# A two-stage block with linear attention and a gated layer: mask, zero products, shifts, numerators and the written-out order changed together

## The chip, the cores and the metric

One Trainium2 chip, one of its cores. The metric is the device time of one execution in microseconds (us), the median of several runs. The core has five engines that run their own instruction queues: TensorE (PE), VectorE (DVE), ScalarE (ACT), GpSimd (POOL) and SyncE (SP), which here issues nearly all DMAs. Matmul results go to PSUM, eight banks of 512 fp32 columns; everything else lives in SBUF.

## The reference

Input `x` is 2048 rows of 640 (bf16). First linear attention with 32 heads of 20 columns, then a bilinear gated layer, each behind a LayerNorm without weights and with a residual. Cut to what matters:

```python
def _A_ref(x, wqkv, w_phi, wo):
    qkv = (x @ wqkv).reshape(B, S, 3, H, Dh).transpose(2, 0, 3, 1, 4)
    q, k, v = qkv[0], qkv[1], qkv[2]
    pq = einsum("bhsd,hdf->bhsf", q, w_phi)
    pk = einsum("bhsd,hdf->bhsf", k, w_phi)
    phi_q = concatenate([softmax(pq), softmax(-pq)], -1)
    phi_k = concatenate([softmax(pk), softmax(-pk)], -1)
    kv = einsum("bhsf,bhsd->bhfd", phi_k, v)
    z = einsum("bhsf->bhf", phi_k)
    num = einsum("bhqf,bhfd->bhqd", phi_q, kv)
    den = einsum("bhqf,bhf->bhq", phi_q, z)[..., None] + 1e-6
    return (num / den).transpose(0, 2, 1, 3).reshape(B, S, D) @ wo
h = x + _A_ref(layernorm(x), A_wqkv, A_w_phi, A_wo)
n = layernorm(h)
out = h + ((n @ B_w_gate) * (n @ B_w_up)) @ B_w_down
```

## The kernel before, in words

**Tiles.** The 2048 rows are 16 tiles of 128. Names of operations carry the tile: `K7` is the key projection of tile 7.

**How the order is set.** `build_graph` makes some thousand operations, each with its engine, reads and writes. Nothing is scheduled at run time: the table `PLAN` gives each operation a due time, which sorts its engine's queue, an optional choice of engine (`:1` or `:2`, an index into the alternatives named at the operation), and the slot that it takes in a pool of buffers (PSUM banks for matmuls). The entry `xn3:12.223:1:2` means: tile 3's normalised rows, twelfth microsecond, second choice of engine, slot 2. `emit` sets the semaphore waits that the order and the reuse of slots ask for. An instruction that waits holds up all behind it on its engine.

**Opening.** PE first runs ten products of zeros, 512 columns each (L365), of which eight touch one PSUM bank each. Meanwhile SP loads `x1`, `x0` and the five row blocks `wk0` to `wk4` of the key weight. GpSimd builds the identity (`id0`, `id1`, L324 and L327) and the block mask `GL`, which tells for each of 128 rows of a weight chunk which head it belongs to: a memset (L325) and two selections for each of the five chunks (`gla`, `glb`, L333 and L336), ten in all. `Ph0` to `Ph2` (L374) multiply the small matrix `w_phi` with that mask into the block matrix Phi. PE transposes the key weight (`WT0` to `WT4`, L386), multiplies it with Phi (`F1_0` to `F1_4`, the folds, L405), and the folded weight then makes features straight from rows. Evacuations from PSUM are `WTe`, `Fe`, `xte`, `Ve` (L245), on ScalarE or VectorE.

**Rows.** Per tile: statistics (`L1s`, `L1a`, VectorE), one over the deviation by logarithm and exponential (`L1l`, `L1e`, ScalarE, for groups of 1, 1, 2, 4, 4 and 4 tiles), the shift -mean times that (`L1n`, L437, one instruction per tile, on GpSimd or VectorE, from tile 2 on), the normalised rows (`xn`, L445 on ScalarE or L447 on VectorE), and their transposition (`xt`: tiles 0 to 3 on PE, L456, the others by a transposing DMA on SP, L465). Tiles 0 and 1 have their projections cut into five pieces by weight block (`V0_0` to `V0_4`).

**Keys and values.** `V` and `K` (L476), two exponentials of plus and minus the product (`Kx`, L488), sums (`Ks`), reciprocals by `Kr` and `Ke`, the product that normalises (`Kn`, GpSimd, L512, 1280 columns), and `KV` (L520), eleven matmuls per tile that gather over all tiles in two PSUM banks. `KVe` masks them into `KVm`.

**Queries.** `wqt` transposes the query weight from memory by DMA, `F0` folds it, and `Q` makes the products; `Qx` the exponentials (L545 and L547) into one of six slots of `ph`; `Qs`, `Qr`, `Qb`, `Qe` the sums and their ratio; `Qn` (GpSimd, L564, 660 columns); `qT` (SP, L569) transposes `ph` and frees its slot when it has landed.

**Numerators.** `N` (L582): eleven matmuls per tile, three heads each, 63 columns (the last 42): 20 numerators and the denominator per head. Groups 0 to 5 lie in one bank, 6 to 10 in another. `dd` and `rd` (L593, L596) make the reciprocal denominators, `o` (L599) the quotients, both as two halves of 18 heads, which is 36 or 720 columns. `oT` transposes by DMA, `O` (L609) multiplies with the output weight, `h` (L615) adds the residual, `hc` centres it, `hT` transposes it.

**Gated layer.** Blocks of 256, 512, 512, 512 and 256 rows: `U` (L652) twice per 128 columns of the inner width, `g` and `u` (L657, L660), `D` (L671), `y` (L683) and the write `w` (L685). The last tile, 15, has its `D` and `y` cut by columns at 320 and 512 (`LASTCUT`).

```python
G.op("pe", "N%d" % t, nf, mm_c(*[21 * n for n in BH]), LT, [phT] + kvm_b, [b], kk)
...
G.op("sp", "qT%d" % t, lambda e, ph=ph, phT=phT: e.dma_start_transpose(
    out=T["phT"][:, phT.slots[0], :, :], in_=T["ph"][:, ph.slots[0], :]), 1.5, 0.0, [ph], [phT], kk, dma=-2.3)
```

Of the kernel before, what the change touches and what calls it, by code (L numbers as in the profile page):

```python
# [32 lines left out]

NB = 11
# [8 lines left out]
NWARM = 10  # L43
LASTCUT = [(0, 320), (320, 512), (512, 640)]
# [4 lines left out]
gl0:0.78 gla2:0.942 phz:1.084 eps:1.8 gla3:1.83 glb3:2.059 zero:0.91 w5:0.78 gla1:2.198 warm0:1.239 x1:0.78 id0:2.34 gla0:2.484 glb2:2.626 gla4:2.765 L1s1:3.188  # L49
L1a1:4.098 L1l1:4.331 x0:1.26 L1s0:4.207 L1a0:5.117 L1e1:4.657 glb4:2.994 xn1:5.226::0 Ph2:3.223 glb0:3.817 glb1:3.955 Ph0:4.184 wk2:1.74:1 L1l0:5.35 L1e0:5.676  # L50
xn0:5.914::1 warm1:1.665 warm2:2.091 warm3:2.517 Ph1:4.778 warm4:2.943 warm5:3.369 warm6:3.795 wk0:2.22:1 x2:2.7 warm7:4.221 warm8:4.647::0 wk1:3.18 warm9:5.077
id1:5.17 WT2:5.52::0 WTe2:6.139 WT0:5.958::1 WTe0:6.724 xt1:6.375::2 xt0:6.654::3 xte0:7.309 F1_2:6.933::4 WT1:7.252::6 WTe1:7.894:1 wk3:3.66 WT3:7.669::7
L1s2:6.426 Fe1_2:7.45 WTe3:8.289 xte1:8.697:1 F1_0:8.086::0 Fe1_0:8.603:1 wk4:4.14:1 WT4:8.405::3 WTe4:9.104:1 F1_1:8.822::4 Fe1_1:9.339 x3:4.62:1 x6:5.1
L1s3:9.512 L1a2:10.3 F1_3:9.141::6 Fe1_3:9.923 va1:5.414 L1a3:10.422 K0_0:9.46::0 L1s6:10.531 F1_4:9.731::2 Fe1_4:10.507:1 L1s7:11.319 wv0:5.58:1 V0_0:10.1::4
wv1:6.06 L1l2:11.091 x4:6.54 K0_1:10.371 K0_2:10.642 L1e2:11.417 L1s5:12.105 ekz:6.244 L1n2:11.697 V1_0:10.913::6 V1_1:11.184 L1n3:11.921 xn3:12.223:1:2
L1s4:12.893 L1a4:13.803 L1a7:13.912 K1_0:11.455::2 x12:7.02 wv2:7.5:1 K1_1:11.726 K0_3:11.997 wv4:7.98:1 L1a5:14.021 xn2:14.13::3 K1_2:12.268 K1_3:12.539
K1_4:12.81 V0_1:13.081 Kx1_0:13.28::0 Kx1_1:13.864 V1_2:13.352 wv3:8.46 wu1:8.94 L1a6:14.642 wg4:9.42 V0_2:13.623 V0_3:13.894 V0_4:14.165 wqt4:9.9 Ve0:14.635::0
V1_3:14.436 xt3:14.707::2 xte3:15.184:1 L1l4:15.219 L1e4:15.545 L1n5:15.825 K0_4:14.986 x8:11.21 Kx0_0:15.638::1 Kx0_1:16.222 Ks1:15.592::0 L1n4:16.049
V1_4:15.257 xt2:15.528::3 K3:15.807::4 Ve1:16.806::1 L1n7:16.985:1 L1n6:16.273 xn6:17.39:1:0 Kr1:18.195 V3:17.163::0 Ke1:18.486 Kn1:18.82 xn4:18.632:1:1
xn7:19.437:1:2 x10:11.69 wqt0:12.17 Ve3:20.242::2 xn5:17.16::3 xt5:17.785 rqz:21.133 xte2:17.672:1 L1s9:18.081 L1s11:18.867 Kx3_0:20.826::2 Kx3_1:21.41  # L60
# [24 lines left out]
V15:71.666::2 Ve15:73.222::5 KV12:73.022 KV13:73.355 KV14:73.688 KV15:74.021 KVe1:74.555 Qb5:73.403 Qe5:73.806 Qr13:73.925::2 Qn5:74.113 Q7:74.354::0
KVe0:74.805 N1:75.721::6 qT5:76.245::0 dd1:76.252::0 rd1:76.467 N0:76.054::2 o1:76.881::0 Q14:76.387::4 Qb13:75.378 Qe13:75.653 Qx7_0:75.919::0 Qx7_1:76.529
dd0:77.692::0 rd0:77.907 Qn13:75.96 oT1:77.808::0 qT13:79.118::1 N3:77.754::0 dd3:78.285::1 rd3:78.5 o0:78.79::1 o3:79.601::2 oT0:80.608::1 oT3:81.918::2
Q11:78.087::6 Qx11_0:79.652::5 Q8:79.746::2 Qx11_1:80.262 Qs7:80.412 N2:81.113::0 dd2:81.847::0 rd2:82.062 Qx14_0:80.872::1 Qx14_1:81.482 O1:81.446::6
o2:82.476::0 oT2:83.403::3 h1:83.287 Qr7:82.092::0 Qb7:82.436 N9:82.804::4 dd9:84.107::0 rd9:84.322 o9:84.736::1 Q12:83.432::0 Qe7:82.711 Qx8_0:83.328::2
N5:84.799::6 dd5:85.547::0 rd5:85.762 o5:86.176::2 Qx8_1:83.938 hc1:84.548::3 O0:85.132::2 h0:86.987 hc0:87.932::2 O3:86.49::4 h3:88.047 N4:87.848::6  # L90
dd4:88.867::0 L2q1:88.65 rd4:89.082 o4:89.496::0 Qn7:83.018 qT7:84.713::4 Qx12_0:89.49::0 Qr6:90.1::1 L2v1:90.307:1 oT9:86.203::0 L2q0:90.246 O2:88.181::2
hT1:87.513 Qb6:90.444 Qe6:91.086 Q15:89.539::4 O9:90.906::6 Qx12_1:91.205 N7:92.264::0 h2:90.392 Qs8:91.212 Qn6:91.393 h9:92.647 dd7:93.467::0 rd7:93.682
# [139 lines left out]
def build_graph():  # L232
# [341 lines left out]
    for t in range(NT):  # L574
# [13 lines left out]
        def nv(b, lo, hi):  # L588
            return pp(b, 0, 378).rearrange("p b (h e) -> p b h e", e=21)[:, :, :, lo:hi]
# [323 lines left out]
```

## Time and profile before

| | us |
|---|---|
| median of three runs (272.31 to 272.6) | 272.32 |
| the profiled execution | 272.55 |
| its span, first to last instruction | 270.8 |
| first product of zeros starts | 1.25 |
| first transposition of a weight starts | 6.03 |
| last matmul ends | 268.28 |

The granted TensorE clock is 1.00 in the whole span. All times below that are given as points are us from the start of the span of the profiled execution. A row of the page or of a stage shows the busy time of each engine and the number of its instructions; a row of a group shows busy time, the mean duration of one instruction in ns, and then the idle time of its engine just ahead of it with what ended that. PE's matmuls overlap: a matmul of 320 columns lasts about 0.30 us in the records, but the next starts 0.136 us after it.

### The profile page before, as it was taken

How to read it: one execution, taken by the hardware profiler on the slowest of the kernel's cores; microseconds unless marked ns; L12 is line 12 of the kernel's file. 1: busy time of each engine (PE TensorE's matmuls, PEld its weight loads, DVE VectorE, ACT ScalarE, POOL GpSimd, SP SyncE). 2: the span in 40 equal slices, each digit the busy share in tenths (PEclk: the TensorE clock that was granted, in tenths of full speed). 3: DMA queues.
4: the chain of work that ended last, by engine and by line, in shares of the span. 5: the costliest groups of instructions: out<-in, count | busy, mean ns of one | idle time of the engine just before them, and what ended most of it. 6: DMA issues, size and time to landing. Idle time of an engine off the chain costs nothing.

```text
span 270.8 us, 5184 instructions
## 1 busy us (share of the span) xinstructions
PE 266.0 (98%) x2103; PEld 177.1 (65%) x2103; DVE 161.6 (60%) x295; ACT 123.8 (46%) x304; POOL 72.8 (27%) x98
## 2 busy tenths in 40 slices
PE   7999999999999999999999999999999999999996
PEld 3877787777777689865656747775445457544774
DVE  4989999989689978887754434223123312424224
ACT  3999999788846667232254443003213510032000
POOL 8124989999942222331000000000000000000000
DMA  6997899967947989589347032041000000100003
GB/s 185 323 249 159 128 299 329 146 140 134 196 91 149 131 180 157 62 167 120 59 91 105 0 73 51 0 69 30 29 0 15 0 0 27 69 5 1 2 24 104
DMA packets 66600, 27.76 MB, mean 103 GB/s; under 512 B 57744, under 2 KB 65296, under 8 KB 66576
## 3 DMA queue, kind: packets, MB, share of 16 engines
q1 hardware_dynamic: 65120, 26.42, 47.3%
q10 hardware_dynamic: 1456, 1.01, 1.6%
q8 instruction: 16, 0.26, 0.4%
q14 instruction: 8, 0.07, 0.1%
HBM read 11.00 MB, written 2.62 MB: 50 GB/s over the span
## 4 chain that ended last, share of the span: by engine, by line
PE 90%; DVE 3%; DMA 3%; ACT 2%; POOL 1%; issue 0%; SPq 0%; DVEq 0%; POOLq 0%
PE ps L652 38%; PE ps L476 22%; PE ps L671 19%; PE ps L609 6%; PE ps L520 2%; DMA scratch<-ph 2%; PE ps L582 1%; DVE o L599 1%; PE ps L405 1%; DMA w<-in_A_w_phi_dram 1%; DVE sm L596 1%; ACT scratch L245 1%; POOL Phi L374 1%; DVE S L550 1%; ACT ph L545 0%; ACT ek L626 0%
## 5 line engine op out<-in xcount | busy, mean ns | idle before, releaser
L652 PE MATMUL ps<-xnT,Wgu 128*128 128x512 bf16 (+1 forms) x600 | 107.0, 336 | 0.0
L652 PEld LDWEIGHTS ps<-xnT,Wgu 128*128 128x128 bf16 x600 | 58.1, 98 | 43.4 <-DVE ev L660 0.4
L657 ACT ACTIVATE gt<-ps 128x512 bf16<-128x512 f32 (+1 forms) x60 | 29.0, 510 | 94.2 <-PE ps L652 90.4
L476 PE MATMUL ps<-Wp,xnT 128*128 128x320 bf16 (+1 forms) x480 | 68.8, 299 | 0.3 <-DVE o L599 0.2
L660 DVE TENSOR_TENSOR ev<-ps,gt 128x512 bf16<-128x512 f32 (+1 forms) x60 | 33.3, 580 | 41.7 <-PE ps L652 28.8
L476 PEld LDWEIGHTS ps<-Wp,xnT 128*128 128x128 bf16 x480 | 45.5, 97 | 18.3 <-DVE o L599 0.7
L671 PE MATMUL ps<-Wd,ev 128*128 128x320 bf16 (+2 forms) x396 | 53.3, 295 | 0.0
L671 PEld LDWEIGHTS ps<-Wd,ev 128*128 128x128 bf16 x396 | 38.1, 98 | 14.8
L512 POOL TENSOR_TENSOR ek<-ek,SR 128x1280 bf16<-128x1280 bf16 x16 | 37.5, 2357 | 4.0 <-ACT SR L497 3.9
L683 DVE SCALAR_TENSOR_TENSOR Wp<-ps,rs,x_all 128x640 bf16<-128x640 f32 (+3 forms) x18 | 14.4, 807 | 38.2 <-PE ps L671 38.1
L550 DVE TENSOR_REDUCE S<-ph 128x66 f32<-128x1320 bf16 x16 | 24.0, 1521 | 3.5 <-ACT ph L547 3.4
L630 POOL TENSOR_SCALAR ln<-mv 128x1 f32<-128x1 f32 x8 | 1.5, 190 | 89.3 <-ACT ek L626 88.9
L492 DVE TENSOR_REDUCE SR<-ek 128x64 f32<-128x1280 bf16 x16 | 23.3, 1478 | 1.2 <-ACT ek L488 1.0
L609 PE MATMUL ps<-Wo,Wp 128*128 128x320 bf16 x160 | 24.0, 299 | 0.0
L564 POOL TENSOR_TENSOR ph<-ph,RQ 128x660 bf16<-128x660 bf16 x16 | 20.8, 1306 | 10.2 <-ACT RQ L560 10.0
L545 ACT ACTIVATE ph<-ps 128x600 bf16<-128x600 f32 x32 | 21.2, 679 | 4.3 <-PE ps L476 3.6
L488 ACT ACTIVATE ek<-ps 128x640 bf16<-128x640 f32 x32 | 21.1, 701 | 0.5 <-PE ps L476 0.5
L609 PEld LDWEIGHTS ps<-Wo,Wp 128*128 128x128 bf16 x160 | 15.4, 98 | 6.7
L615 DVE SCALAR_TENSOR_TENSOR x_all<-ps,x_all 128x640 bf16<-128x640 f32 x16 | 13.1, 820 | 9.3 <-PE ps L609 9.2
L599 DVE TENSOR_TENSOR o<-ps,sm 128x720 bf16<-128x720 f32 x16 | 14.4, 903 | 1.3 <-DVE sm L596 0.5
L626 ACT ACTIVATE ek<-x_all,mv 128x640 bf16<-128x640 bf16 x16 | 13.1, 821 | 2.8 <-DVE x_all L615 2.8
L624 ACT ACTIVATE xn<-x_all,mv 128x640 bf16<-128x640 bf16 x10 | 8.2, 825 | 9.5 <-DVE x_all L615 9.5
(64 smaller groups left out, 166.3 us busy)
## 6 DMA issues: line engine op xcount, KB each, us to landing
out_dram<-Wp SPq DMA_DIRECT2D x15, 160.0 KB, 1.9
x_all<-in_A_x_dram SPq DMA_DIRECT2D x6, 320.0 KB, 6.1
Wgu<-in_B_w_up_dram SPq DMA_DIRECT2D x5, 384.0 KB, 6.4
Wgu<-in_B_w_gate_dram SPq DMA_DIRECT2D x5, 384.0 KB, 4.1
Wd<-in_B_w_down_dram SPq DMA_DIRECT2D x2, 480.0 KB, 6.8
Wd<-in_B_w_down_dram ACTq DMA_DIRECT2D x2, 480.0 KB, 4.5
ev<-in_A_wqkv_dram SPq DMA_DIRECT2D x5, 160.0 KB, 3.8
Wp<-in_A_wqkv_dram SPq DMA_DIRECT2D x5, 160.0 KB, 5.9
```

The costliest lines, as they stand in the source:

```text
L476: ins = e.matmul(pb(b, hb)[:, 0:n1 - n0], lhsT=T["xnT"][:, NC - 1 - c, P * t:P * (t + 1)], rhs=T["Wp"][:, POS[kind], c, n0:n1], start=(c = ...
L488: G.op("act", "%sx%d_%d" % (nm, t, s), lambda e, s=s, b=b, ek=ek: e.activation(out=T["ek"][:, ek.slots[0], 0:2 * D].rearrange("p (b h s f) ...
L492: G.op("dve", "%ss%d" % (nm, t), lambda e, ek=ek, sr=sr: e.tensor_reduce(out=T["SR"][:, sr.slots[0], 0, :], in_=T["ek"][:, ek.slots[0], 0: ...
L512: G.op("pool", "Kn%d" % t, lambda e, eng, ek=ek, sr=sr: e.tensor_tensor(out=T["ek"][:, ek.slots[0], 0:2 * D].rearrange("p (h f) -> p h f", ...
L545: e.activation(out=v[:, 0:10].rearrange("p (b g) j f -> p b g j f", b=2), in_=pp(b, 0, 300).rearrange("p b (g j f) -> p b g j f", j=3, f=D ...
L550: G.op("dve", "Qs%d" % t, lambda e, t=t, ph=ph: e.tensor_reduce(out=T["S"][:, t, 0:66].rearrange("p (g k) -> p g k", k=6), in_=pv(ph).rear ...
L564: return e.tensor_tensor(out=v, in0=v, in1=T["RQ"][:, rq.slots[0], 1, 0:33].rearrange("p (g j) -> p g j", j=3).unsqueeze(3).to_broadcast([ ...
L609: ins = e.matmul(pb(b, hb)[:, 0:320], lhsT=T["oT"][:, oT.slots[0], c, :], rhs=T["Wo"][:, c, 320 * hb:320 * (hb + 1)], start=(c == 0), stop ...
L652: ins = e.matmul(pb(b)[:, 0:n], lhsT=T["Wgu"][:, gu, c, P * ft:P * (ft + 1)], rhs=T["xnT"][:, NC - 1 - c, o0:o0 + n], start=(c == 0), stop ...
L657: G.op("act", "g%d_%d" % (bi, ft), lambda e, pg=pg, gt=gt, n=n: e.activation(out=T["gt"][:, gt.slots[0], 0:n], in_=pb(pg)[:, 0:n], func=AF ...
L660: o_ = G.op("dve", "u%d_%d" % (bi, ft), lambda e, pu=pu, gt=gt, hh=hh, ft=ft, n=n: e.tensor_tensor(out=T["hh"][:, hh.slots[0], ft, 0:n], i ...
L671: ins = e.matmul(pb(b, hb)[:, 0:w], lhsT=T["hh"][:, hh.slots[0], ft, P * tt:P * (tt + 1)], rhs=T["Wd"][:, ft, c0 + w * hb:c0 + w * (hb + 1 ...
```

## The change

Seven things change together.

1. The mask gets one layout for all chunks, nine columns per chunk (`GW`), and is made by a memset and two selections over all 45 columns; the products that make Phi read the columns that they need from it.
2. The zero products are 256 columns wide instead of 512: eight that touch the banks and fourteen more (`NFILL`), the last two of them among the first transpositions. The memset that they read is half as large.
3. The shift `L1n` is one VectorE instruction per group of tiles instead of one instruction per tile on GpSimd or VectorE.
4. The numerators of group g start at column 64 g of two neighbouring banks (eight groups in the first, three in the second), and `dd`, `rd` and `o` run over 11 groups of three heads: 33 instead of 36, and 660 instead of 720 columns.
5. `xn` may run on GpSimd; `PLAN` puts tiles 2, 3, 4, 7, 9, 11 and 13 there. Before, 3, 4 and 7 were on ScalarE and the others on VectorE.
6. The last tile is cut at 320 and 576 instead of 320 and 512; its middle part, now 256 columns, is still the last matmul group of all.
7. `PLAN` is new from end to end: due times, slots and some choices of engine for evacuations, loads and the second LayerNorm.

The diff, cut; of `PLAN` the lines of the opening and those around tile 7's transposition:

```diff
+GW = 9
...
-NWARM = 10
-LASTCUT = [(0, 320), (320, 512), (512, 640)]
+NFILL = 14
+LASTCUT = [(0, 320), (320, 576), (576, 640)]
...
-dd4:88.867::0 L2q1:88.65 rd4:89.082 o4:89.496::0 Qn7:83.018 qT7:84.713::4 Qx12_0:89.49::0 Qr6:90.1::1 L2v1:90.307:1 oT9:86.203::0 L2q0:90.246 O2:88.181::2
-hT1:87.513 Qb6:90.444 Qe6:91.086 Q15:89.539::4 O9:90.906::6 Qx12_1:91.205 N7:92.264::0 h2:90.392 Qs8:91.212 Qn6:91.393 h9:92.647 dd7:93.467::0 rd7:93.682
...
+xt1:6.093::2 xte1:6.571 xn0:6.114::1 gl0:1.526 gla:1.688 wk1:2.22 wk2:2.7:1 WT1:6.372::3 WT2:6.651::4 xt0:6.93::5 glb:1.992 Ph2:2.585 Ph0:3.179 WTe2:7.154
+WTe0:6.644:1 Ph1:3.773 F1_0:7.209::6 Fe1_0:7.739:1 WTe1:7.052 warm21:7.528 F1_1:7.637::0 Fe1_1:8.323 wk4:3.18:1 WT4:7.956::2 x3:3.66:1 wk3:4.14 WT3:8.235::3
...
+V1_0:11.639::2 K0_2:11.91 K0_3:12.181 wv1:6.54 V0_1:12.452 K0_4:12.723 V1_1:12.994 L1a6:14.56 wv2:7.02:1 V0_2:13.265 Kx0_0:13.193::1 Kx0_1:13.777 Ks0:14.669::0
+xn2:11.908:2:2 xt2:13.536::4 wv3:7.5 V0_3:13.815 x10:7.98 wv4:8.46:1 V0_4:14.086 xte2:14.361 xn3:13.008:2:3 L1l4:14.945 L1e4:15.271 L1n4:16.062 xn5:16.296::0
...
+Qe7:82.235 Qn7:82.542 Q15:84.24::4 qT7:84.321::0 oT9:85.811::0 N5:85.607::2 dd5:86.138::0 rd5:86.353 Qx14_0:84.421::1 Qx14_1:85.031 N4:85.94::6 dd4:86.643::1
+hc1:85.641::0 hT1:87.121 o5:86.767::2 Q12:86.273::0 O2:87.664::2 hc0:86.359::2 hT0:88.431 rd4:87.522 o4:87.936::0 Qx12_0:88.531::4 Qx12_1:89.141 Qs8:88.691
+Qr8:90.244::3 Qb8:90.588 Qe8:90.863 oT4:89.741::1 h2:90.126 Qn8:91.17 O3:89.022::6 hc2:91.071::1 h3:90.946 O9:90.38::0 h9:91.937 N7:91.738::2 dd7:92.757::0
...
-    for c in (0, 4, 1, 2, 3):
-        lo, n, o = CH[c][0], NH[c], OFF[c]
-        base = P * c - DH * lo
-        k = -97 if c in (0, 4) else -80
-        G.op("pool", "gla%d" % c, lambda e, n=n, o=o, base=base: e.affine_select(
-            out=T["GL"][:, o:o + n], in_=T["GL"][:, o:o + n], compare_op=ALU.is_ge, fill=0.0, base=base,
-            pattern=[[-DH, n]], channel_multiplier=1), 0.22, LP, [gl_b[c]], [gl_b[c]], k)
...
+    G.op("pool", "gla", lambda e: e.affine_select(
+        out=T["GL"][:, :, :], in_=T["GL"][:, :, :], compare_op=ALU.is_ge, fill=0.0, base=0, pattern=[[P - 6 * DH, NC], [-DH, GW]],
+        channel_multiplier=1), 0.24, LP, [gl_b], [gl_b], -97)
+    G.op("pool", "glb", lambda e: e.affine_select(
+        out=T["GL"][:, :, :], in_=T["GL"][:, :, :], compare_op=ALU.is_ge, fill=0.0, base=DH - 1,
+        pattern=[[6 * DH - P, NC], [DH, GW]], channel_multiplier=-1), 0.24, LP, [gl_b], [gl_b], -96.5)
...
+    for k in range(8):
+        G.op("pe", "warm%d" % k, lambda e, k=k: e.matmul(T["PS"][:, 512 * k:512 * k + 256], lhsT=T["zero"][:, 0:P],
+             rhs=T["zero"][:, :], start=True, stop=True), 0.11, LT, [z_b], [], -90,
+             before=[G.by["warm%d" % j] for j in range(k)])
...
-                G.op("pool", "L1n%d" % t, lambda e, eng, t=t: e.tensor_scalar(
-                    out=T["nb"][:, t:t + 1], in0=T["mv"][:, t, 0:1], scalar1=T["rs"][:, t:t + 1], scalar2=-1.0, op0=ALU.mult,
-                    op1=ALU.mult), 0.2, LP, [rs_b[t], mv_b[t]], [nb_b[t]], 10 * t - 25, alts=[("dve", 0.07, LD)])
+        if z > 2:
+            G.op("dve", "L1n%d" % a, lambda e, a=a, z=z: e.scalar_tensor_tensor(
+                out=T["nb"][:, a:z], in0=T["mv"][:, a:z, 0], scalar=-1.0, in1=T["rs"][:, a:z], op0=ALU.mult, op1=ALU.mult), 0.075, LD,
+                [rs_b[t] for t in tl] + [mv_b[t] for t in tl], [nb_b[t] for t in tl], 10 * a - 25)
...
-             alts=[] if t < 2 else [("act", act_c(640, True), LA)])
+             alts=[] if t < 2 else [("act", act_c(640, True), LA), ("pool", 1.15, LP)])
...
-                y, h0, h1 = g // 6, 3 * g, 3 * g + BH[g]
-                ins = e.matmul(pb(b, y)[:, 21 * (h0 - 18 * y):21 * (h1 - 18 * y)], lhsT=T["phT"][:, phT.slots[0], g, :],
+                y, h0, h1 = g // 8, 3 * g, 3 * g + BH[g]
+                ins = e.matmul(pb(b, y)[:, 64 * (g % 8):64 * (g % 8) + 21 * BH[g]], lhsT=T["phT"][:, phT.slots[0], g, :],
...
-            out=T["o"][:, o.slots[0], :].rearrange("p (b h d) -> p b h d", b=2, d=DH), in0=nv(b, 0, 20),
-            in1=smv(sm, 1).unsqueeze(3).to_broadcast([P, 2, 18, DH]), op=ALU.mult), dve_c(720, True), LD, [b, sm], [o], kk)
+            out=T["o"][:, o.slots[0], 0:33 * DH].rearrange("p (g j d) -> p g j d", j=3, d=DH), in0=nv(b, 0, 20),
+            in1=smv(sm, 1).unsqueeze(3).to_broadcast([P, NB, 3, DH]), op=ALU.mult), dve_c(660, True), LD, [b, sm], [o], kk)
```

In the new `PLAN`, PE's order from Q7 on is Q7, N1, N0, Q11, N3, Q8, N2, N9, Q14, O1, O0, Q15, N5, N4, Q12, O2, O3, O9, N7, U0. ScalarE's around it: Qx7 twice, Qr10, the first half of Qx11, Qr6, Qe6, the second half of Qx11. SP's: qT5, oT1, oT0, qT13, oT3, oT2, qT7, oT9, hT1, hT0. SP's loads at the start: x1, x0, wk0, wk1, wk2, wk4, x3, wk3, x2, wv0, x6, x4, wv1, wv2, wv3, x10, wv4 (x6, x4 and x10 are two tiles each); before: x1, x0, wk2, wk0, x2, wk1, wk3, wk4, x3, x6, wv0, wv1, x4, x12, wv2, wv4, wv3.

## The prediction

> **What bounds the kernel now.** First the page's busy times, then TensorE (PE) by stages, from the first transposition of a weight (6.03) to the end of the last matmul. In each row the figure after the comma is PE's busy time.
>
> ```profile
> PE 266.0 (98%) x2103; PEld 177.1 (65%) x2103; DVE 161.6 (60%) x295; ACT 123.8 (46%) x304; POOL 72.8 (27%) x98
> ...
> 6.03:16.57 10.54, 10.47 (x115) 8.32 (x116) 9.28 (x27) 8.94 (x19) 1.73 (x4) 1.00 1.15 299
> 16.57:76.89 60.32, 60.32 (x605) 45.16 (x603) 54.37 (x68) 53.26 (x141) 51.01 (x46) 1.00 0.83 188
> 76.89:94.40 17.51, 16.85 (x189) 12.22 (x186) 16.28 (x34) 10.68 (x30) 4.22 (x5) 1.00 0.87 138
> 94.40:268.29 173.89, 173.88 (x1194) 110.03 (x1194) 78.49 (x161) 48.90 (x112) 10.82 (x21) 1.00 0.30 55
> ```
>
> PE is full in the second and fourth row, and there the matmuls start at their own pace: 136 ns apart for 320 columns, 216 for 512, 31 for 63. Busy time hides waits shorter than a matmul's 0.2 to 0.6 us, so I read the start of every matmul and took the pace off. After 6.03 about 2.1 us are lost: 0.25 in WT0, 0.24 before F1_1, 0.16 before V0_0, 0.16 before V0_3, then 0.27 before Q8, 0.37 before Q12, 0.55 before N7 and 0.12 before U0; 0.2 more is spread over 2000 matmuls. Only four places can be shortened: the start, the opening, the stage around 77 to 94, and what follows the last matmul (2.5 us). The chain of waits names them:
>
> ```profile
> 5.64 0.26 POOL ident L327
> 5.90 0.14 issue
> 6.03 0.70 PE ps L386 x5
> ...
> 86.03 5.30 DMA scratch<-ph
> 91.33 0.02 issue
> 91.35 0.67 ACT ph L545
> ...
> 268.38 0.42 DVE Wp L683
> ```
>
> The start hangs on GpSimd (POOL), which makes the identity last, after ten selections and three products. Later one transposition of feature rows, qT7, takes 5.30 us; only then is its `ph` slot free for Qx12, which must empty the banks that N7 needs. The last write ends the program.
>
> **Sum against the profiled execution:** it took 272.55 us, of which 270.8 are the span; the median of the runs shown is 272.32. I work out a difference in the span and take it off the median.
>
> **The opening.** Ten selections become two (L333/L336 took 0.19 to 0.20 us for 7 or 8 columns, the mask's L353 0.31 for 33; two times 0.2 to 0.31), and id0, id1, eps and `ekz` (0.62) come ahead, `phz` (0.84) and `va1` (1.23) behind Phi. So the identity is ready near 2 instead of 5.89. Phi's three products (1.8) still wait for w5, landed at 3.47, and end near 5.3. The zero products: 22 of 256 columns instead of 10 of 512. The ten started 0.427 us apart, half the full pace, so 20 take 4.27 and end near 5.4 (they start 0.12 earlier, the memset being half as large). Then WT0 needs wk0, now third on SP's queue; the third landing was at 5.28. So dense work starts near 5.45, 0.58 earlier. The two last zero products (0.1 to 0.2 each) fall into gaps: xt1 still waits for xn1 on VectorE (DVE), which ended at 6.20.
>
> I don't book 0.58, because **what is late next** is weights. SP's order changes, but the queue delivers one 160 KB tile per 0.4 to 0.9 us: the 20th landed at 14.60 (wv3, which V0_3 waited for). In the new order the 20th is wv4, for V0_4. PE alone gets there at about 14.2: 5.45, five WT and two xt at 0.28 (2.0), xt2 (0.28), five folds at 0.32 (1.6), sixteen projection pieces at 0.272 (4.35), zero products 0.3, and about 0.25 at half pace. Waits of up to 0.4 (Fe1_1 behind four evacuations of 0.59 on ScalarE) are thus covered; beyond that they cost in full. V0_4 at 14.66, four pieces (1.09) and xt3 (0.28) give V2 at 16.03. The same work was done before at K3, 16.57: **-0.54** (0 to -0.95).
>
> **Rows on GpSimd.** Seven `xn` (2, 3, 4, 7, 9, 11, 13) go there from ScalarE (0.92 each) and DVE (0.55 to 0.60). No such row exists. From below: GpSimd's tensor-scalar of one column, 0.19. From above: its product of 1280 columns.
>
> ```profile
> L512 POOL TENSOR_TENSOR ek<-ek,SR 128x1280 bf16<-128x1280 bf16 x16 | 37.5, 2357 | 4.0 <-ACT SR L497 3.9
> L564 POOL TENSOR_TENSOR ph<-ph,RQ 128x660 bf16<-128x660 bf16 x16 | 20.8, 1306 | 10.2 <-ACT RQ L560 10.0
> ```
>
> The nearest row, 660 columns, makes 1.27 for 640; I take that. xn2 can start near 12.3, after DVE's new shift; xt2 may come at 14.1 and xt3 at 15.75 without delaying V0_4 or V2, so 1.7 each is free, behind V0 and V1 on PE. The other five queue among the Kn products. From 16.57 to 76.89 GpSimd is idle for 9.3 us, 3.9 of it early, waiting for ScalarE before a Kn; ten L1n (0.27 each) leave, so 8.0 can be used, and five rows take 6.4. Booked at nothing; if that cover goes, KV15 is late by the rest. Four shifts of about 0.2 go to DVE, which PE didn't wait for there.
>
> From 16 to 76 I book **0**: same matmuls, no PE wait before, evacuations at similar distances. The tightest spot is F0_1, which needs wqt0: SP reaches it after xt5 (near 17.5; 1.3), x14 (0.6) and five more transpositions (1.3 each), near 25.9; wqt1 took 4.1 us to land, so 30.0. Ten projections at 1.36 and two KV at 0.34 from V2's start put F0_1 at 30.3.
>
> **The stage at 77 to 94.** Numerators at a stride of 64 leave N's eleven matmuls as they are; o shrinks from 720 to 660 columns (0.903, less 60 columns at 1.25 ns: 0.83), rd and dd by three columns (0.02). Nine tiles: 0.8 of the 16.28 us that DVE is busy. Bounds: -0.8 to 0 (the pattern gains a dimension; the old one also crossed a bank); I take 0, since the SP queue, not DVE, is late here. Before, 1.31 were lost. In the new order N9 needs the banks of Q11, whose second exponential stands behind Qe6. By rows from the end of Q7: start 0.2, two exponentials at 0.63, Qr10 0.26, Qb10 0.24, Qn13 1.27, Qb6 0.24, Qe6 0.23, exponential 0.7: 4.45, while PE has four N and two Q, 4.08. Loss 0.4. Then qT7 again: Qx12 waits for its slot, and O9 now needs Q12's banks.
>
> ```profile
> q8 instruction: 1, 0.02, 0.6%
> ...
> scratch<-ph SPq DMA_TRANSPOSE x1, 5.3
> ```
>
> This is the DMA view of 84 to 94. The eight qT before it took 3.50 to 3.80; in qT7's time one 16 KB instruction packet ran (88.88 to 89.80). Sixteen such packets come, one per 77 to 167 matmuls, and transpositions under way lose 0.8 to 1.8 us. The Trainium skill (Runtime: NRT & Kernel Launch, Instruction fetch mechanics) says that engines refill instructions in 16 KiB blocks and that the cost is mostly hidden; here the trace disagrees as to who pays, the transposition: 5.3 against 3.6. By the page's rule the loss before O9 would be 0.
>
> With twelve more matmuls at the start, the packet after the 857th now falls into N5, 1.7 us after qT7's issue: it hits again. From that issue O9 is due in about 5.9 (Q15, N5, N4, Q12, O2, O3), less 1.3 for Qx12: 4.6 allowed. At 3.55 no loss, at 5.30 0.7. I take 0.5. Together 0.9 instead of 1.31: **-0.41** (-1.0 to +0.5, the latter if hT0 on the packed SP queue also comes late for U0).
>
> **The end.** D15's rest is cut 256+64 instead of 192+128: **+0.02** on PE. Its last evacuation has 256 columns: rows 0.349 at 128, 0.418 at 192, 0.553 at 320 give 0.49, +0.07; the write lies between 1.51 (192) and 1.58 (320), +0.04: **+0.11**.
>
> **Sum:** -0.54 -0.41 +0.02 +0.11 = -0.82. 272.55 becomes 271.73, the median 272.32 becomes **271.5**.
>
> **Rivals.**
> - *New waits eat the gain* (0.25): F0_1 late by 0.4 behind wqt0, or the full 0.7 before O9 with U0 late too: 271.9 to 272.5, the same. For it: SP is packed and the margins from qT5, qT13 and qT7 to their slots are alike short. Against: in 16 to 76 PE never waited.
> - *No collision* (0.12): qT7 at 3.6 and wv4 sooner: 270.8 to 271.0.
> - *GpSimd rows too long* (0.06; slower): from 1.85 us each. Then xt3 is late by 0.35 (12.3 + 3.7 + 0.1 against 15.75), and five rows make 9.25, 1.25 more than the queue has free before KV15: 273.1. At the 2.36 of the largest row 1.35 and 3.8: 276.6. Against: the nearest row says 1.27. The Trainium skill (GPSIMD Engine Reference, 3.1 Elementwise) gives about one cycle of 1.2 GHz per element for one input; an estimate from it, with 0.19 for the start, is 0.74, which leaves the sum as it is.
> - *Full clock late* (0.04; slower). The ten zero products and WT2 and WT0 ran at half pace, the transpositions of xt1 (7.04) at full, 5.7 us after the first matmul. If half pace lasted until the folds end, near 10.4, some 2.6 us of work would take twice as long, less 0.4 covered: 273.7. The Trainium skill (TensorE: Matmul & The Clock Gate, Part 1) has a free-running window of about 3.4 us that must be busy, counted in time, not in matmuls; by that the smaller products do as well. The trace agrees: full pace between one and two windows after the first matmul.
> - *The change does nothing* (0.02): PE's work is the same, and waits not seen here take back each gain; 272.3.
>
> **Chances.** Forecast 0.51. A measurement of this kernel can't tell less than 0.2% (0.54 us) from no change. Faster: 0.49 of the forecast's cases and the third's 0.12, 0.61; same: 0.02, 0.25 less 0.01, and 0.02, 0.28; slower 0.11. The range takes in no collision below and the new waits above, 270.6 to 272.7.
>
> **What would show it.** Right: WT0 at 5.4 to 5.5; V0_4 near 14.65 and V2 near 16.0; GpSimd's rows at 1.1 to 1.4; waits before N9 (0.4) and O9 (0.5); PE's last matmul ending near 267.4; 2.6 after it. Wrong: PE waits between 16 and 76, GpSimd rows above 1.55, xt1's transpositions still 107 ns apart after 8 us, or U0 waiting for hT0.

## The result, and the profile after

The changed kernel takes 276.3 us (median of four runs, 276.04 to 276.64) beside 272.44 for the kernel before on the same chip: ratio 1.0142, 95% interval 1.0125 to 1.0160. It is slower; the forecast was 271.5. The profiled execution took 276.36, its span is 274.6.

The page's busy times:

```profile
PE 265.0 (97%) x2100; PEld 178.2 (65%) x2115; DVE 161.0 (59%) x297; ACT 120.9 (44%) x297; POOL 86.3 (31%) x85
```

The rows by stages, cut where TensorE (PE) waited; the figure after the comma is PE's busy time, POOL is the last with a count:

```profile
5.35:19.00 13.65, 11.97 (x131) 9.12 (x131) 12.92 (x33) 11.25 (x23) 8.93 (x7) 1.00 1.07 267
19.00:33.41 14.41, 12.77 (x111) 9.16 (x110) 11.72 (x22) 11.52 (x26) 13.09 (x9) 1.00 0.65 109
33.41:43.70 10.29, 9.94 (x124) 7.88 (x124) 8.87 (x16) 7.95 (x20) 10.29 (x6) 1.00 0.83 187
43.70:53.90 10.20, 9.39 (x94) 6.92 (x95) 10.20 (x9) 9.03 (x28) 10.20 (x6) 1.00 0.63 160
53.90:81.00 27.10, 27.10 (x263) 20.11 (x264) 21.16 (x18) 20.15 (x64) 25.39 (x23) 1.00 0.98 221
```

PE starts earlier (WT0 at 5.35), but loses time up to 54 us, where nothing was to be lost; from there it is full again. GpSimd (POOL) has 86.3 us instead of 72.8. From 33 to 54 it has no pause at all (10.29 of 10.29, 10.20 of 10.20). The groups of instructions say what took the time, and the chain of waits where it ended up:

```profile
L510 POOL TENSOR_TENSOR ek<-ek,SR 128x1280 bf16<-128x1280 bf16 x16 | 37.5, 2356 | 1.6 <-ACT SR L495 1.6
L562 POOL TENSOR_TENSOR ph<-ph,RQ 128x660 bf16<-128x660 bf16 x16 | 20.8, 1309 | 13.7 <-ACT RQ L558 13.5
L445 POOL TENSOR_SCALAR xn<-x_all,mv,rs 128x640 bf16<-128x640 bf16 x7 | 17.5, 2503 | 4.7 <-DVE nb L435 4.7
```

```profile
11.82 0.07 DVE nb L435
11.90 0.10 issue
12.00 5.01 POOL xn L445 x2
17.00 0.05 issue
17.05 0.45 PE ps L454 x5
...
47.08 2.50 POOL xn L445
49.57 0.02 issue
49.59 4.24 DMA xnT<-xn
53.83 0.04 issue
53.88 5.62 PE ps L474 x40
```

One row costs 2.50 us, twice the 1.27 of the forecast, and more than the product of twice its width (2.36). xn2 and xn3 run from 12.00 to 17.00, so the transpositions xt2 and xt3 wait, and xn13 ends at 49.57, so K13 waits until 53.88.

The longest wait came by way of SP, whose queue the next view shows (start, length, what was issued). It reaches xt7 after 18.9, but xn7 is the fourth row in a stretch on GpSimd and ends at 21.97. Behind it stand xt4, xt6 and three weight transpositions, the last of them wqt0:

```profile
18.32 0.58 SPq L281 DMA_DIRECT2D x_all<-in_A_x_dram  x1
21.99 3.85 SPq L463 DMA_TRANSPOSE xnT<-xn  x3
25.88 3.90 SPq L305 DMA_TRANSPOSE scratch<-in_A_wqkv_dram  x3
```

wqt0 lands at 33.37, and F0_1 starts at 33.41. The start of each matmul less the start of the one before and less its pace gives what PE lost: xt2 1.10, xt3 0.86, F0_1 1.82, K11 0.53, K13 0.95, N9 0.49, O2 0.17. The first five make 5.26.

### The profile page after: what moved, and what is told of

It is laid out like the page before. It is cut to its first block, busy times and chain, and to the rows that moved or that the text cites. A ratio compares the mean times of both kernels' runs of the same rounds, so it can differ in the third digit from the quotient of the medians.

```text
span 274.6 us, 5192 instructions
## 1 busy us (share of the span) xinstructions
PE 265.0 (97%) x2100; PEld 178.2 (65%) x2115; DVE 161.0 (59%) x297; ACT 120.9 (44%) x297; POOL 86.3 (31%) x85
## 3 DMA queue, kind: packets, MB, share of 16 engines
HBM read 11.00 MB, written 2.62 MB: 50 GB/s over the span
## 4 chain that ended last, share of the span: by engine, by line
PE 78%; POOL 10%; DMA 5%; issue 2%; SPq 2%; ACT 1%; DVE 1%; DVEq 0%
PE ps L653 37%; PE ps L672 17%; PE ps L474 12%; PE ps L610 8%; POOL ek L510 5%; POOL xn L445 5%; PE ps L580 2%; DMA x_all<-in_A_x_dram 2%; SPq L281 2%; DMA xnT<-xn 2%; DMA out_dram<-Wp 1%; ACT ek L486 1%; PE ps L518 1%; DVE Wp L684 0%; DVE st L421 0%
## 5 line engine op out<-in xcount | busy, mean ns | idle before, releaser
L653 PE MATMUL ps<-xnT,Wgu 128*128 128x512 bf16 (+1 forms) x585 | 105.7, 335 | 0.7
L658 ACT ACTIVATE gt<-ps 128x512 bf16<-128x512 f32 (+1 forms) x60 | 29.7, 510 | 91.3 <-PE ps L653 68.1
L672 PE MATMUL ps<-Wd,ev 128*128 128x320 bf16 (+2 forms) x396 | 54.2, 295 | 0.0
L445 POOL TENSOR_SCALAR xn<-x_all,mv,rs 128x640 bf16<-128x640 bf16 x7 | 17.5, 2503 | 4.7 <-DVE nb L435 4.7
L600 DVE TENSOR_TENSOR o<-ps,sm 128x660 bf16<-128x660 f32 x16 | 13.5, 844 | 0.6
```

The lines of the kernel that those rows point to most:

```text
L445: return e.tensor_scalar(out=rev(xb), in0=T["x"][:, t, :].rearrange("p (c n) -> p c n", c=NC), scalar1=T["mv"][:, t, 0:1], scalar2=T["rs"] ...
L653: ins = e.matmul(pb(b)[:, 0:n], lhsT=T["Wgu"][:, gu, c, P * ft:P * (ft + 1)], rhs=T["xnT"][:, NC - 1 - c, o0:o0 + n], start=(c == 0), stop ...
L658: G.op("act", "g%d_%d" % (bi, ft), lambda e, pg=pg, gt=gt, n=n: e.activation(out=T["gt"][:, gt.slots[0], 0:n], in_=pb(pg)[:, 0:n], func=AF ...
L672: ins = e.matmul(pb(b, hb)[:, 0:w], lhsT=T["hh"][:, hh.slots[0], ft, P * tt:P * (tt + 1)], rhs=T["Wd"][:, ft, c0 + w * hb:c0 + w * (hb + 1 ...
```

## The experiments

In all of them "the row" is an `xn` on GpSimd, and the loss of a wait is what a matmul's start lies behind the start of the one before it, less the pace.

**1. All seven rows back on their old engines.**

```diff
-xn2:11.908:2:2   xn3:13.008:2:3   xn4:16.346:2:1   xn7:17.446:2:2
+xn2:11.908::2    xn3:13.008:1:3   xn4:16.346:1:1   xn7:17.446:1:2
-xn11:26.173:2:1  xn9:29.586:2:3   xn13:42.436:2:2
+xn11:26.173::1   xn9:29.586::3    xn13:42.436::2
```

> The changed kernel with its seven GpSimd rows put back where they were before (xn3, xn4, xn7 on ScalarE, xn2, xn9, xn11, xn13 on VectorE), at the same places of the order; all else as changed. Theory A (the 2.50 us rows are the whole loss): the waits before xt2 1.10, xt3 0.86, F0_1 1.82, K11 0.53 and K13 0.95 go, 5.3 us of 276.3: 271.0 to 271.6, and the waits before N9 (0.5) stay. Theory B (the new order of SP's queue makes wqt0 and the row transpositions late, whoever makes the rows): xt2 and xt3 go, F0_1, K11 and K13 stay: 274.0 to 274.6. Theory C (the rows only change places: ScalarE and VectorE get 3.0 and 2.3 us more in a packed opening): evacuations late, 272.3 to 273.5.

Measured: 274.41, ratio 1.0068 (1.0054 to 1.0083). This is 1.9 better, not 5.3. The time is theory B's, but the trace isn't: xt2, xt3, F0_1, K11 and K13 wait no more. New waits stand in their place: V3 0.75, Q3 1.34, V2 0.33, K7 0.24; N9 0.48 as before. V3's is theory C's: its bank is emptied on ScalarE behind three rows in a stretch (17.43 to 19.87). Q3's was foreseen by no theory. Here is the chain that leads to it:

```profile
37.88 1.49 DVE SR L490
39.37 2.08 DVE nb L435
41.44 0.03 issue
41.47 0.04 DVE xn L445
...
41.99 0.60 DVE xn L445
42.59 0.74 DVE Wp L247
43.33 0.05 issue
43.38 1.67 PE ps L474 x11
```

L435 is the new group-wise shift, 128 partitions of four columns on VectorE (DVE). It takes 2.08 us. Here are its durations (shortest, middle, longest, in ns), and then GpSimd's line of the time:

```profile
L435 DVE SCALAR_TENSOR_TENSOR nb<-mv,rs x4: 153/536/2149, 11.5 to 39.3; 128x4 f32<-128x4 f32 x3, 128x2 f32<-128x2 f32 x1
```

```profile
36.74 6.98 POOL L510 TENSOR_TENSOR ek<-ek,SR 128x1280 bf16<-128x1280 bf16 x3 [0.81 <-ACT SR L495]
```

The same instruction takes 0.15 at its shortest and 2.15 at its longest. By the records of single instructions the long ones end 15 to 20 ns after a `Kn` product on GpSimd: 41.43 after one at 41.41, 25.85 after 25.83; in the changed kernel 25.80 after 25.79. I formed theory D from this: a VectorE instruction with two tensors in SBUF waits for the GpSimd product in hand.

**2 and 3. Two halves of it.** The same edit for five rows, then for the other two.

```diff
 xn2, xn3 as changed; xn4, xn7 to ScalarE; xn9, xn11, xn13 to VectorE
```

> The changed kernel with only the five later rows put back (xn4 and xn7 on ScalarE, xn9, xn11 and xn13 on VectorE); xn2 and xn3 stay on GpSimd. Theory A: xt2 and xt3 still wait 1.10 and 0.86, the three later waits (1.82, 0.53, 0.95) go: 273.0, F0_1 without a wait. Theory B: F0_1 still waits for wqt0, at 33.4 as in the changed kernel: 275.5 to 276.4. Theory C: about as A plus up to 1: 273.5 to 274.

Measured: 274.84, ratio 1.0088 (1.0073 to 1.0104). No theory's time came. xt2 and xt3 wait 0.94 and 0.85, F0_1 doesn't: theory B falls. Again Q3 waits, 1.25, and again the shift takes 2.15; without Q3's wait the time would be 273.6, theory C's.

```diff
 xn2 to VectorE, xn3 to ScalarE; the five others as changed
```

> The changed kernel with only xn2 (VectorE) and xn3 (ScalarE) put back; the five later rows stay on GpSimd. Theory A, with one deadline behind the other: TensorE gains the 1.96 us of xt2 and xt3, but F0_1 is set by the absolute time at which SP gets past xt7, which waits for xn7; xn4 can start at 16.4 instead of 17.0, so xn7 ends 0.6 sooner and F0_1 starts near 32.8, after a wait of about 3.2 instead of 1.8: 275.7. If the five waits simply add up: 274.4. Theory B: as the first, with wqt0 issued near 28.5 whatever xn7 does: 276.2.

Measured: 277.13, ratio 1.0165 (1.0126 to 1.0204), four runs far apart (274.98 to 278.46), so the median says little. The profiled run is the fastest of them, 1.4 below the profiled run of the changed kernel. There F0_1 starts at 32.40 (foreseen 32.8), after a wait of 1.50 (foreseen 3.2), with 0.53 before V7 and 0.44 before KV0. Of the 1.96 gained at xt2 and xt3, 1.0 is left at F0_1, which started at 33.41 in the changed kernel. Half of the early gain is lost by the next deadline: the waits don't add up.

**4. What a row on GpSimd costs.** One kernel with forms of it, three times each.

```diff
+e.tensor_scalar(out=rev(k), in0=x, scalar1=mv, scalar2=rs, op0=sub, op1=mult)     # L73
+e.tensor_scalar(out=xn, ... the same without reversal)                            # L75
+e.tensor_scalar(out=xn, in0=x, scalar1=0.5, scalar2=2.0, op0=sub, op1=mult)       # L77
+e.tensor_scalar(out=xn, in0=x, scalar1=mv, op0=sub)                               # L79
+e.tensor_scalar(out=xn, in0=x, scalar1=0.5, op0=mult)                             # L81
+e.tensor_tensor(out=xn, in0=x, in1=x1, op=mult)                                   # L83
+... L75's form on 320 (L85) and 1280 columns (L87), a copy (L89)
```

> No attention and no projection: a load, then forms of a row on GpSimd three times each, VectorE idle but in the last group, and x is written out. On 128x640 bf16: (1) as in the changed kernel (two operations, per-partition scalars, chunks in reverse), (2) the same without the reversal, (3) two operations with constants, (4) one operation with a per-partition scalar, (5) one with a constant, (6) a product of two tensors, (7) form 2 on 320 columns, (8) form 2 on 1280, (9) a copy, (10) form 2 from fp32, (11) form 1 while VectorE works on rows of its own. If GpSimd makes one pass per operation: 1, 2, 3 near 2.5, 4 and 5 near 1.3, 7 near 1.3, 8 near 4.9. If the per-partition scalars cost it: 3 and 5 near 1.2, 4 above 1.8. If the reversal costs it: 1 2.5 and 2 near 1.3. If VectorE slows it: 1 near 1.3 and 11 near 2.5.

The groups of that kernel, busy time and mean ns behind the bar:

```profile
L87 POOL TENSOR_SCALAR big<-x_all,mv,rs 128x1280 bf16<-128x1280 bf16 x3 | 14.0, 4679 | 0.0
...
L75 POOL TENSOR_SCALAR xn<-x_all,mv,rs 128x640 bf16<-128x640 bf16 x3 | 7.5, 2502 | 0.0
L73 POOL TENSOR_SCALAR xn<-x_all,mv,rs 128x640 bf16<-128x640 bf16 x3 | 7.5, 2502 | 9.2 <-DMA x_all<-in_A_x_dram 9.2
L77 POOL TENSOR_SCALAR xn<-x_all 128x640 bf16<-128x640 bf16 x3 | 7.0, 2350 | 0.0
L79 POOL TENSOR_SCALAR xn<-x_all,mv 128x640 bf16<-128x640 bf16 x3 | 5.6, 1883 | 0.0
L81 POOL TENSOR_SCALAR xn<-x_all 128x640 bf16<-128x640 bf16 x3 | 5.4, 1811 | 0.0
L85 POOL TENSOR_SCALAR xn<-x_all,mv,rs 128x320 bf16<-128x320 bf16 x3 | 4.3, 1435 | 0.0
L83 POOL TENSOR_TENSOR xn<-x_all 128x640 bf16<-128x640 bf16 x3 | 4.1, 1392 | 0.0
L89 POOL COPY xn<-x_all 128x640 bf16<-128x640 bf16 x3 | 2.0, 721 | 0.0
```

Reversal costs nothing (L73 against L75), per-partition scalars little (0.15), the second operation 0.54 to 0.62, far less than the first. The tensor-scalar form is slow in itself: with one operation 1.81, more than the product of two tensors (1.39). From 320 to 640 columns it is 3.3 ns a column. A row from fp32 took 2.50 too; beside VectorE rows 2.78.

The Trainium skill (GPSIMD Engine Reference, 3.1 Elementwise), which the prediction cited for one input, puts a two-input operation at about 2.6 cycles an element and a port-bound body at about one. At its 1.2 GHz that makes 1.39 and 0.55, estimates; the product (1.39) agrees, the copy (0.72) is 0.17 longer. The tensor-scalar row agrees with neither: it has one input and takes 2.50.

**5. The short row.** Everything as changed, but a row leaves out half of its columns, so that it lasts about as long as was forecast.

```diff
+out=rev(xb)[:, :, 0:64], in0=x[...][:, :, 0:64]      # on GpSimd alone
```

> The changed kernel, every step at its place, but the seven GpSimd rows normalise only 64 of each 128 columns (the other half of those rows is left out; two slots are zeroed once on the idle VectorE). By the forms measured a row then takes about 1.44 us, near the 1.27 of the prediction. Theory A (the prediction was wrong in the length of this row alone): 271.3 to 271.8, no wait before F0_1, K11, K13. Theory D (besides, the group-wise shift on VectorE, a two-tensor instruction, waits for the GpSimd product that is running: 2.15 us instead of 0.15 in the run with the rows put back, where Q3 then waited 1.34): Q3 waits about 1.3 here too: 272.6 to 273.1.

Measured: 273.94, ratio 1.0065 (1.0051 to 1.0080). The rows took 1.43. F0_1's wait falls from 1.82 to 0.36 and xt2, xt3, K11 and K13 have none, but Q3 waits 1.40, as theory D has it, and KV0 0.90, which it hadn't foreseen. Two shifts took 1.88 and 2.15, until a product on GpSimd ended; the chain to Q3 goes through the second, which holds up VectorE's queue. The size of the row alone was not the whole mistake.

**6. The short row and another shift.** One tensor input and a per-partition scalar, for ScalarE's rows only. Rows on the other engines, which don't read the shift, no longer wait for it either.

```diff
-G.op("dve", "L1n%d" % a, ... scalar_tensor_tensor(out=nb[:, a:z], in0=mv[:, a:z, 0], scalar=-1.0, in1=rs[:, a:z], ...)
+G.op("dve", "L1n%d" % t, ... tensor_scalar(out=nb[:, t], in0=mv[:, t, 0], scalar1=rs[:, t], scalar2=-1.0, ...)
```

> The same short GpSimd rows (half of their columns left out), and the shifts are made on VectorE by one instruction with one tensor input for each of the two rows that ScalarE makes (xn6, xn10), instead of four two-tensor ones. Theory D: no shift waits for GpSimd, the Q3 wait goes: 1.0 to 1.4 below the run with short rows alone, 271.3 to 271.8. If the shift's wait cost nothing there: the same as that run within 0.2.

Measured: 272.07, ratio 0.9990 (0.9978 to 1.0002). 1.9 less than without the edit, more than foreseen, since KV0's wait went as well as Q3's. The new shifts took 0.20 each, the second of them (24.59) beside a product on GpSimd, and VectorE's row behind it kept its usual 0.60 there:

```profile
L437 DVE TENSOR_SCALAR nb<-mv,rs 128x1 f32<-128x1 f32 x2 | 0.4, 200 | 0.0
```

```profile
22.19 4.67 POOL L515 TENSOR_TENSOR ek<-ek,SR 128x1280 bf16<-128x1280 bf16 x2 [3.38 <-ACT SR L500]
...
24.71 0.60 DVE L450 TENSOR_SCALAR xn<-x_all,mv,rs 128x640 bf16<-128x640 bf16 x1
```

What of the 1.9 is the shorter shift and what the freed rows was not parted; the chain of experiment 5 names the shift itself.

**7. The fourth cell: long rows, other shift.**

```diff
 rows as in the changed kernel; shifts as in 6 (xn6 and xn10 alone)
```

> The changed kernel with its 2.50 us GpSimd rows, and only the shifts replaced: one-input instructions on VectorE for xn6 and xn10, no two-tensor shift. The fourth cell beside the changed kernel (276.3), short rows (273.9) and short rows with these shifts (272.1). If rows and shifts each add their own loss: 276.3 less 1.9, 274.4. If the rows are the later of the two everywhere but at xn13, which waited for the shift on GpSimd: K13's 0.95 goes and little else: 275.3 to 275.8. If the shift's wait only shows where the rows are short: 276.3.

Measured: 276.58, ratio 1.0144 (1.0121 to 1.0168), the changed kernel's own. This is the third outcome: with long rows the shift's wait is hidden (K13 then waits 1.33, and F0_1 still 1.49); with short rows it is worth 1.9. The four cells: 1.0142 and 1.0144 with long rows, 1.0065 and 0.9990 with short ones.

**8. The wait by itself.** Five forms on VectorE, alone and beside three kinds of GpSimd instruction.

```diff
+V: scalar_tensor_tensor 128x4 (two tensors) | tensor_scalar 128x4 | tensor_tensor 128x640 | tensor_scalar 128x640 | copy 128x640
+G: nothing | tensor_tensor 128x1280 x8 | tensor_scalar 128x1280, two operations x5 | copy 128x1280 x12
```

> No attention and no projection: a load, five forms on VectorE in turn, five times, with GpSimd idle, then beside 1280-column products on GpSimd, then beside its 1280-column two-operation rows, then beside its copies. Forms: (1) two SBUF tensors of 128x4, (2) one of 128x4 with a per-partition scalar, (3) product of two 128x640, (4) a 128x640 row with per-partition scalars, (5) a 128x640 copy. Theory D: beside the products 1 and 3 wait for the end of the product in hand (up to 2.3 us, mean above 1), 2, 4 and 5 don't; beside the two-operation rows 1 stays near 0.15, as it did once in the changed kernel. If the shift's length had another cause: all five forms keep their idle durations beside products. If GpSimd slows VectorE in general: all five get longer.

In order of time, first beside products (POOL's line holds six of 2.7), then beside two-operation rows (three of 4.8):

```profile
17.44 0.16 DVE L95 SCALAR_TENSOR_TENSOR a<-f 128x4 f32<-128x4 f32 x1 [0.28 <-POOL big L68]
17.45 16.20 POOL L70 TENSOR_TENSOR g<-x_all 128x1280 bf16<-128x1280 bf16 x6
17.52 2.57 DVE L96 TENSOR_SCALAR a<-f,mv 128x4 f32<-128x4 f32 x1
20.01 0.48 DVE L97 TENSOR_TENSOR b<-x_all 128x640 bf16<-128x640 bf16 x1
20.41 2.71 DVE L98 TENSOR_SCALAR b<-x_all,mv,rs 128x640 bf16<-128x640 bf16 x1
23.05 2.72 DVE L99 COPY b<-x_all 128x640 bf16<-128x640 bf16 x1
25.68 2.55 DVE L95 SCALAR_TENSOR_TENSOR a<-f 128x4 f32<-128x4 f32 x1
```

```profile
42.61 14.46 POOL L74 TENSOR_SCALAR g<-x_all,mv,rs 128x1280 bf16<-128x1280 bf16 x3
...
47.41 0.31 DVE L107 COPY b<-x_all 128x640 bf16<-128x640 bf16 x1
47.64 0.15 DVE L103 SCALAR_TENSOR_TENSOR a<-f 128x4 f32<-128x4 f32 x1
47.72 4.50 DVE L104 TENSOR_SCALAR a<-f,mv 128x4 f32<-128x4 f32 x1
```

Alone the five took 0.15, 0.22, 0.48, 0.44 and 0.32. The first shift (17.44) began just ahead of the first product and took 0.16; the next one, beside a product, takes 2.55, until that ends. VectorE's own product shows 0.48, but it always begins just as one of GpSimd's ends, and GpSimd's next then takes 2.91 in its record instead of 2.62 to 2.68; so it seems to go first. Beside GpSimd's copies of 1.25 the four forms that waited here take 1.17 to 1.37. Against theory D, the forms with one input wait as well (2.57, 2.71, 2.72). Beside a two-operation row the two-tensor shift doesn't wait (0.15; in the changed kernel it took 0.16, 1.7 us after such a row had begun), while the 128x4 form with one input does (4.50). The copy at 47.41 doesn't either (0.31), though a row had begun at 47.30.

The Trainium skill (SBUF — State Buffer, Who interferes with whom) says that VectorE and GpSimd share a port pair, held for a whole instruction: VectorE needs it with two SBUF inputs against GpSimd instructions that read SBUF, and in its two-port modes, which copies and tensor-scalar forms can enter. GpSimd's products and copies agree. Its two-operation row differs: it reads SBUF, and the two-tensor shift passed it. The measurement decides; of the forms that began during such a row only the one-tensor 128x4 form was held up, and the 640-column product and row never began in the middle of one. Nor do all tensor-scalar forms on VectorE wait beside a product: the 128x1 shifts (0.20) and the rows with reversed chunks (0.60) of experiment 6 didn't. What sets them apart from the forms tried here was not tested.

**9. A version without both costs.** One row on GpSimd, where 2.5 us are free, and the one-input shifts.

```diff
 xn7 as changed (GpSimd); xn3, xn4 to ScalarE; xn2, xn9, xn11, xn13 to VectorE; shifts as in 6
```

> The whole computation: of the seven rows only xn7 stays on GpSimd, where it can start near 16.6 and end near 19.1, when SP reaches xt7; xn3 and xn4 go to ScalarE and the other four to VectorE, and the shifts are made on VectorE by one-input instructions, for ScalarE's five rows only. Against the run with all seven put back (274.4): theory D takes off the 1.34 before Q3; and if V3's wait of 0.75 there came from the three rows in a stretch on ScalarE, it goes as well: 272.3. Only theory D: 273.1. Neither: 274.4. If xn7 on GpSimd is too late for xt7, F0_1 waits for wqt0: up to 273.5.

Measured: 272.35, ratio 0.9996 (0.9984 to 1.0008). The waits before V3, Q3, xt2, xt3 and F0_1 are gone. Left are V0_4 1.29 (wv4 landed at 15.47), K11 0.32 and N9 0.48. The time is the one foreseen if both waits go. What remains of the change is worth nothing that can be told.

**10 and 11. The waits that are left.**

```diff
-x10:7.98 wv4:8.46   +wv4:7.98 x10:8.46                                       # 10, and 11 as well
-xt10:32.074 wg1:33.384 xt11:33.864   +xt11:32.074 xt10:33.384 wg1:34.694     # 11
-Qe6:78.864 Qx11_1:78.983   +Qx11_1:78.983 Qe6:79.62                          # 11
```

> The kernel with xn7 alone on GpSimd and one-input shifts (272.35), with one exchange in SP's queue: the weight tile wv4 ahead of the activation tiles x10. By the prediction's step on the opening V0_4 waits for wv4, which lands 0.4 to 0.9 after the tile ahead of it; in that kernel's profile it waited 1.29 (wv4 at 15.47), in others 0.4. If that wait counts in full: 0.4 to 0.9 less, 271.5 to 271.9. If V2's or F0_1's operands are late next: 272.2 to 272.4.

Measured: 272.55, ratio 1.0001 (0.9987 to 1.0015). No gain, and neither outcome's time. V0_4 waits no more, but V2 (0.33) and F0_1 (0.31) do. By the gated layer (U0) the profiled run is still 0.74 ahead of that of experiment 9; there it loses 0.99 before O8:

```profile
PE ps L611 <- DMA Wp<-o: 0.8, 1, 0.8
```

O8 waits for oT8, whose transposition took 6.33 (112.46 to 118.79), with a 16 KB instruction packet under way (112.84 to 113.76). In the profiled run of experiment 9 the packet came before that transposition, which took 3.1.

> The same with two more exchanges: the transposition xt11 ahead of xt10 and of the weight wg1 on SP (K11 waited 0.32 to 0.48 for it, K10 is used 4.7 us later), and on ScalarE Qe6, which waits for two GpSimd steps, behind the second exponential of Q11, so that N9's banks come free. By the prediction's reading of the stage at 77 to 94 the wait before N9 (0.48) was that exponential behind Qe6. Both go: 0.8 to 0.96 below the kernel with wv4 first: 270.6 to 271.1. If N9 then waits for what comes before it on ScalarE: 0.3 to 0.5 less only, 271.1 to 271.5.

Measured: 272.01, ratio 0.9986 (0.9975 to 0.9998): the fastest of all, by 0.14%, less than the 0.2% that the prediction set as the least that can be told. It is 0.5 below experiment 10; 0.8 to 0.96 were foreseen if both waits go. N9's and K11's waits are gone, so the reading of that stage was right; F0_1 (0.68) and Q14 (0.32) took back half. Its rows by stages:

```profile
5.45:30.66 25.21, 24.55 (x241) 18.44 (x240) 24.78 (x58) 23.05 (x47) 12.43 (x10) 1.00 0.88 204
30.66:76.56 45.90, 45.90 (x475) 34.61 (x476) 40.16 (x42) 37.95 (x110) 40.56 (x31) 1.00 0.88 209
76.56:94.00 17.44, 17.28 (x195) 12.76 (x193) 15.34 (x32) 11.44 (x32) 6.08 (x8) 1.00 0.78 141
```

PE is full from F0_1 to 76.56, where N1 starts, which did so at 76.73 before: of the 0.58 gained at the start (dense work from 5.45, before from 6.03) 0.17 is left.

**12. Weight transpositions in SP's gap.**

```diff
-wqt4:22.654 wqt1:23.964 xte2:14.361   +wqt4:12.7 wqt1:14.0 xte2:13.776
```

> The kernel of the last run (272.0) with SP's two weight transpositions wqt4 and wqt1 taken out of the packed stretch ahead of wqt0 and put into the 4 us at 13 to 17.5 in which SP waited for xn5, and on ScalarE the evacuation xte2 one exponential sooner, since V2 waited 0.33 for it. If F0_1's wait (0.31 to 0.68) is the SP queue, as the prediction's step on 16 to 76 has it, and V2's is that exponential: 0.6 to 1.0 less, 271.0 to 271.4. If the two transpositions only push other transfers (x8, x12 and x14 late for the statistics): no gain or up to 0.5 slower, 272.0 to 272.5. If PE's gain is taken back at Q14 and O2 (0.3 and 0.2 there): 271.4 to 271.7.

Measured: 272.20, ratio 0.9997 (0.9987 to 1.0007). No gain. wqt0 lands at 26.96 instead of 30.61 and F0_1's wait is gone, so SP's queue was its cause. But PE comes to F0_1 at 30.66, as in experiment 11, since WT0 (0.49) and V3 (0.53, behind rows and evacuations on ScalarE) have made it late; V2's 0.33 stays, and O2 waits 0.28.

## Why the prediction was wrong

- **The failed step: "Rows on GpSimd", "the nearest row, 660 columns, makes 1.27 for 640; I take that".** Measured 2.50. The nearest row in width was another kind of instruction. The upper bound named there, 2.36, was itself too low. By the prediction's own slack (1.7 for each of two rows, 8.0 for five) 2.50 would have cost 1.6 and 4.5; PE lost 1.96 at xt2 and xt3 and 3.30 behind, 5.26 where 0 was booked.
- **The rival "GpSimd rows too long" was what happened, at a chance of 0.06.** It gave 276.6 at 2.36 us; 276.3 came at 2.50. That the figures lie so close is luck. Its first place was about right (1.35 forecast, 1.96 measured); its second was not. It had KV15 late by what GpSimd's queue lacked; the lateness came sooner, through SP's queue behind xt7, and PE was full from 54 to 81.
- **A second step failed unseen: "Four shifts of about 0.2 go to DVE, which PE didn't wait for there".** Two of the four took 0.64 and 0.95 in the changed kernel and up to 2.15 in the variants. Hidden by the rows in the changed kernel, this cost 1.9 where the rows were about as short as forecast (1.43): 273.9. Had the row been what I took it for, the forecast would still have been some 2 us off. With short rows and the other shifts 272.07 came, inside the range, 0.6 above the forecast.
- **"From 16 to 76 I book 0"** named F0_1 as the tightest spot, by wqt0, at 30.0 against 30.3: there the longest wait came, though SP stood behind xt7 and not behind its own work. The spot was too tight even without the long rows: in experiments 10 and 11 wqt0 landed at 30.67 and 30.61, and F0_1 waited 0.31 and 0.68.
- **Opening (-0.54): right as a mechanism.** WT0 at 5.35 (forecast 5.45). In the run with short rows and other shifts V0_4 started at 14.72 and V2 at 16.10 (forecast 14.66 and 16.03). But V0_4, V2, F0_1 and K11 stand so close that gains there are taken back: the rival "new waits eat the gain".
- **Stage at 77 to 94: right in part.** N9 waited 0.48 (0.4; the terms listed there add up to 4.40 rather than 4.45). qT7 took 4.42 in the changed kernel and 4.0 to 4.6 in the variants, neither 3.55 nor 5.30, and not above the 4.6 allowed: O9 didn't wait (0.5 forecast), O2 did by 0.17 (not forecast).
- **"Full clock late" fell:** WT0 lost 0.10 to 0.68 in all, mostly a wait for wk0 (landed 5.30 to 5.64), and xt1 at most 0.31.
- **Tail: right.** From the last matmul's end to the span's end 2.53 before, 2.66 to 2.68 in eight variants (forecast 0.11 more), but 2.79 and 2.81 in experiments 5 and 9 and 2.84 in the changed kernel's profile. The last matmul ended at 267.68 in experiment 6 and at 267.44 in 11 (forecast 267.4; before 268.28). o took 0.845 (0.83).

Open: whether the opening or the new numerators alone would gain in the old order. This was not tried; all variants from experiment 9 on keep both and stand between 0.9986 and 1.0001.

## What to carry to other kernels

Price an operation that no row shows by its kind before its width: here a tensor-scalar row with two operations on GpSimd cost 1.8 times the product of the same width, and my "nearest" row was the wrong kind. When an instruction moves to an engine, ask not only what stands in its queue but what the neighbour holds while it runs: a shift of four columns took 2.15 us. In a packed order waits hide one another, so a part's cost is read only with the others taken away.

## What the runs showed of the hardware

- GpSimd, 128x640 bf16: copy 0.72, product 1.39, tensor-scalar with one operation 1.81 to 1.88, with two 2.35 to 2.50 (VectorE 0.60 for such a row).
- Beside a product of 1280 columns on GpSimd, four VectorE forms with all operands in SBUF lasted until it ended: a two-tensor 128x4 instruction (2.55 instead of 0.15), a one-tensor 128x4 one (2.57 instead of 0.22), a 128x640 row (2.71 instead of 0.44) and a copy (2.72 instead of 0.32). Others kept their length: 128x1 shifts (0.20), rows with reversed chunks (0.60), and o, which reads PSUM (0.840 beside products, 0.845 apart).
- Beside a two-operation tensor-scalar on GpSimd a two-tensor VectorE instruction of 128x4 ran in 0.15, a one-tensor one in 4.50.
- With a 16 KB instruction packet under way the transposition oT8 took 6.33 in one profile; in another, without one, 3.1.
- The same load, SP's 17th, landed at 13.61, 14.32, 14.68 and 15.47 in four profiles with the same loads ahead of it.
